# A decode step of attention and a gated FFN: the cache read by position blocks of one batch instead of by heads

## The chip, the core and the metric

The kernel runs on one core of a Trainium2 chip. The metric is device time in microseconds from one launch to its end; lower is better. Engines that matter here: PE (matmuls, with its weight loads PEld), DVE (elementwise work and reductions), ACT (copies out of PSUM, exponentials), SP (issues nearly all DMAs) and the 16 DMA engines that move HBM data into SBUF.

## The reference

Four batch rows, one new token each, 32 heads of 192, a cache of 8,192 positions of which the last W = 2,048 are used; D = 640, F = 1,536; everything is bfloat16.

```python
xn = layernorm(x)                                   # x: [4, 1, 640]
q = (xn @ wq) as [4, 32, 1, 192]                    # wq: [640, 6144]
k, v = k_cache[:, :, -W:, :], v_cache[:, :, -W:, :] # [4, 32, 2048, 192] each
p = softmax(q . k * 192 ** -0.5)
attn = (p . v) as [4, 1, 6144] @ wo                 # wo: [6144, 640]
ffn = (silu(xn @ w1) * (xn @ w3)) @ w2              # w1, w3: [640, 1536], w2: [1536, 640]
out = x + attn + ffn
```

The cache lies in HBM as [batch, head, position, 192]. K and V of the window are 201 of the 223 MB that the kernel reads, and each value is used once.

## The kernel before, in words

**Unit of work.** A unit is one head for all four batches. `load_k` and `load_v` (L105 to L113) bring 3 MB each: a partition is (position group q of 32, batch b), and holds 64 positions of 192, a run of 24,576 bytes in HBM. K and V have three buffers each (`kpool`, `vpool`); a load waits until the last reader of its buffer is done.

**Scores.** With one query row per head there is no matrix to multiply, so DVE multiplies K by the broadcast query (`mult`, L228, half a unit or 32 positions at a time), PE sums the products over the 192 elements by 12 accumulating matmuls with an identity (`adder`, L238, 512 columns of 32 positions by 16), and DVE reduces the last 16 (`reduce_tile`, L253). The query is broadcast over partitions by `q_bcast` (L221, L223).

**Softmax.** Per pair of heads: a maximum over a partition's columns (L258), a transpose by PE (L263), the maximum per batch (L268, L271), its broadcast by PE (L277, L279), the exponential on ACT (L283), and `chain_z` (L291), which spreads the weights of a partition over four columns, one for each batch, with zeros in the three that aren't its own. So 16 chains in all.

**Values.** `pv` (L313) multiplies z of eight positions (32 columns) by V of eight positions and 64 of the 192 elements (512 columns), three such column groups of 32 at once. Of the result only the diagonal blocks are wanted: `pick` (L323) masks on DVE and `pick_sum` (L331) adds. `fold` (L338, L344) sums over groups on PE and scales by the row sums; `ge_tr` and `ge_proj` (L350, L357) transpose four heads' result and multiply it by the 768 rows of Wo that belong to them (`wo_load`, L117, 7,680 bytes in a partition, eight times).

**What sets the order.** A table of slots (`sched`, L398 to L454): each stage has a slot number (two slots to a head) and a phase in it, and `behind` (L244) keeps DVE's small work behind the multiply of the same slot. SP's queue runs in program order, so a load that waits for a buffer holds up the loads behind it.

**Start and end.** Wq comes first (three loads, L136), then three K units. At the end: the last V, w1 and w3 (L365), the last Wo, and w2 in loads of 4, 4, 3 and 1 rows in a partition (L372). Behind the last landing stand two matmuls (L467), the final sum (L470) and two small stores (L472, L473).

Of the kernel before, what the change touches and what calls it, by code (L numbers as in the profile page):

```python
# [18 lines left out]
def kernel(  # L19
# [14 lines left out]
    HG: int = 4,  # L34
    QP: int = 8,
    KBUFS: int = 3,
    VBUFS: int = 3,
    PBUFS: int = 2,
    L: int = 7,
    ALIGN: int = 144,  # L40
):

# [12 lines left out]
    NQ = P // B  # L55
    NJ = W // NQ
# [4 lines left out]
    MASK = -30000.0  # L61
    NS = H * NC
    HH = 2
    PL = 32 // B
    DV = 512 // PL
    NV = Dh // DV
    RPP = (HG * Dh) // P
    OW = HG * Dh
    NCH = 512
    QW = 512  # L70
    QB = QP * Dh // QW
    FC = F // P
    DH = D // 2
    assert NJ % CH == 0 and CH * DD <= 512 and QP * Dh % QW == 0
    assert OW % P == 0 and Dh % RPP == 0 and H % HG == 0 and HG % HH == 0 and H % QP == 0 and QP % HH == 0
    assert NV * 32 <= P and NJ % (2 * PL) == 0 and DV * NV == Dh
    NG = P // 32
    NF = F // NCH
    CF = NCH // P
    NB = H * Dh // QW // NG  # L80
    assert H * Dh % (QW * NG) == 0 and NB <= 3
    assert DH <= 512 and F % NCH == 0 and NF <= NG

    const = ctx.enter_context(tc.tile_pool(name="const", bufs=1))
    kpool = ctx.enter_context(tc.tile_pool(name="kt", bufs=KBUFS))
    vpool = ctx.enter_context(tc.tile_pool(name="vt", bufs=VBUFS))
    wpool = ctx.enter_context(tc.tile_pool(name="wstream", bufs=2))
    ppool = ctx.enter_context(tc.tile_pool(name="pr", bufs=PBUFS))
    qpool = ctx.enter_context(tc.tile_pool(name="qbc", bufs=2))
    opool = ctx.enter_context(tc.tile_pool(name="o", bufs=2))  # L90
    small = ctx.enter_context(tc.tile_pool(name="small", bufs=3))
    ps_add = ctx.enter_context(tc.tile_pool(name="ps_add", bufs=2, space=MemoryType.PSUM))
    ps_o = ctx.enter_context(tc.tile_pool(name="ps_o", bufs=1, space=MemoryType.PSUM))
# [3 lines left out]
    kts, vts, prs, pss, scs, zts = {}, {}, {}, {}, {}, {}  # L97
    qbcs, wos, o_pss, rss, rcps, o_rs, o_bfs, chs = ({} for _ in range(8))
    mult_insts, es, o_ms = {}, {}, {}
    ORDER_DEP = mybir.DependencyInfo(mybir.DependencyClass.NoSync, mybir.DependencyReason.SCHED_ONLY)  # L100

    def cache_rows(cache, h):
        return cache[:, h, Sk - W:Sk, :].rearrange("b (q n) d -> q b (n d)", q=NQ)

    def load_k(j):  # L105
        kt = kpool.tile([P, NJ, Dh], BF16, tag="kt")
        nc.sync.dma_start(out=kt[:], in_=cache_rows(A_k_cache, j))
        kts[j] = kt

    def load_v(j):  # L110
        vt = vpool.tile([P, NJ, Dh], BF16, tag="vt")
        nc.sync.dma_start(out=vt[:], in_=cache_rows(A_v_cache, j))  # L112
        vts[j] = vt  # L113

    def wo_load(hg):
        wt = wpool.tile([P, RPP * D], BF16, tag="w")
        nc.sync.dma_start(out=wt[:], in_=A_wo[hg * OW:(hg + 1) * OW, :].rearrange("(p i) n -> p (i n)", i=RPP))  # L117
        wos[hg] = wt

    x_sb = ppool.tile([B, D], BF16, tag="pr")  # L120
    x_rows = A_x.rearrange("b s d -> (b s) d")
    nc.scalar.dma_start(out=x_sb[:], in_=x_rows)
# [7 lines left out]
    RV = NJ * Dh // (H * Dh)  # L130
    wq_rows = A_wq.rearrange("(p kc) n -> p kc n", kc=KC)
    wqs = []
    for r0 in range(0, KC, RV):
        r1 = min(r0 + RV, KC)
        wt = vpool.tile([P, RV, H * Dh], BF16, tag="vt")
        nc.sync.dma_start(out=wt[:, 0:r1 - r0, :], in_=wq_rows[:, r0:r1, :])  # L136
        wqs.append(wt)
    for h in range(KBUFS):
        load_k(h)
# [6 lines left out]
    nc.vector.memset(pad[:, 0:1], 0.0)  # L146
    nsc = const.tile([HH, HH], FP32, name="nsc")
    nc.vector.tensor_scalar_mul(out=nsc[:], in0=idf[0:HH, 0:HH], scalar1=-SCALE)
    selm = const.tile([P, B], FP32, name="selm")
    nc.vector.tensor_reduce(out=selm[:], in_=idf[:].rearrange("p (q b) -> p b q", b=B), axis=AX.X, op=ALU.add)  # L150
    selb = const.tile([P, B], BF16, name="selb")
    nc.vector.tensor_copy(out=selb[:], in_=selm[:])
    row = const.tile([P, 32], FP32, name="row")
    nc.vector.tensor_reduce(out=row[:], in_=idf[:].rearrange("p (g c) -> p c g", g=NG), axis=AX.X, op=ALU.add)
    fsel = const.tile([P, NV, B], FP32, name="fsel")
    nc.vector.tensor_reduce(out=fsel[:], in_=idf[:, 0:NV * 32].rearrange("p (k l b) -> p k b l", k=NV, l=PL), axis=AX.X, op=ALU.add)
    diag = const.tile([P, HH, PL], FP32, name="diag")
    for hh in range(HH):
        nc.vector.tensor_reduce(out=diag[:, hh, :], in_=row[:].rearrange("p (l b) -> p l b", b=B), axis=AX.X, op=ALU.add)
    oTs = []  # L160
    for i in range(2):
        oT = const.tile([P, RPP, 32], BF16, name=f"oT{i}")
        nc.gpsimd.memset(oT[:], 0.0)
        oTs.append(oT)

    xf = ppool.tile([B, D], FP32, tag="pr")
    nc.vector.tensor_copy(out=xf[:], in_=x_sb[:])
    ssum = const.tile([B, 1], FP32, name="ssum")
    nc.vector.tensor_reduce(out=ssum[:], in_=xf[:], axis=AX.X, op=ALU.add)
    negmean = const.tile([B, 1], FP32, name="negmean")  # L170
    nc.vector.tensor_scalar_mul(out=negmean[:], in0=ssum[:], scalar1=-1.0 / D)
    xc = ppool.tile([B, D], FP32, tag="pr")
    nc.vector.tensor_scalar_add(out=xc[:], in0=xf[:], scalar1=negmean[:, 0:1])
    ssq = const.tile([B, 1], FP32, name="ssq")
    nc.scalar.activation(out=xf[:], in_=xc[:], func=ACTF.Square, accum_out=ssq[:])
# [6 lines left out]
    xn = ppool.tile([B, D], BF16, tag="pr")  # L182
    nc.vector.tensor_scalar_mul(out=xn[:], in0=xc[:], scalar1=rstd[:, 0:1])

    xnT_ps = ps_t.tile([P, KC, B], BF16, tag="t")
    for kc in range(KC):
        nc.tensor.transpose(out=xnT_ps[:, kc, :], in_=xn[:, kc:D:KC], identity=idb[0:B, 0:B])
# [4 lines left out]
    sel = const.tile([P, NQ, B], BF16, name="sel")  # L192
    nc.vector.tensor_copy(out=sel[:], in_=selm[:].unsqueeze(1).to_broadcast([P, NQ, B]))

# [3 lines left out]
    for k in range(NB):  # L198
        if k < 2:
            qp = ps_add.tile([P, QW], FP32, tag="ps")  # L200
        else:
            qt = ps_o.tile([P, HH, QW], FP32, tag="o_ps")
            qp = qt[:, 0, :]
        q_pss.append(qp)
    for kc in range(KC):
        for k in range(NB):
            for g in range(NG):
                off = (k * NG + g) * QW
                nc.tensor.matmul(q_pss[k][32 * g:32 * g + 32, :], lhsT=xnT[:, kc, :],  # L209
                                 rhs=wqs[kc // RV][:, kc % RV, off:off + QW], start=(kc == 0), stop=(kc == KC - 1))  # L210
    q_sb = const.tile([P, NB, QW], BF16, name="q_sb")
    for k in range(NB):
        nc.scalar.copy(out=q_sb[:, k, :], in_=q_pss[k][:, :])

    def q_bcast(qg, m):
        k, g = (qg * QB + m) // NG, (qg * QB + m) % NG
        if m == 0:
            qbc = qpool.tile([P, QP, Dh], BF16, tag="qbc")
            qbcs[qg] = qbc
        bp = ps_t.tile([P, QW], FP32, tag="t")  # L220
        nc.tensor.matmul(bp[:], lhsT=sel[32 * g:32 * g + B].rearrange("k q b -> k (q b)"),  # L221
                         rhs=q_sb[32 * g:32 * g + B, k, :], start=True, stop=True)
        nc.scalar.copy(out=qbcs[qg][:].rearrange("p h d -> p (h d)")[:, m * QW:(m + 1) * QW], in_=bp[:])  # L223

    def mult(s):
        j, c = s // NC, s % NC
        pr = ppool.tile([P, CH, Dh], BF16, tag="pr")
        mi = nc.vector.tensor_tensor(out=pr[:], in0=kts[j][:, c * CH:(c + 1) * CH, :],  # L228
                                     in1=qbcs[j // QP][:, j % QP, :].unsqueeze(1).to_broadcast([P, CH, Dh]),
                                     op=ALU.mult)  # L230
        prs[s] = pr
        mult_insts[s] = mi

    def adder(s):
        ps = ps_add.tile([P, CH, DD], FP32, tag="ps")
        pr = prs.pop(s)
        for kk in range(NK):
            nc.tensor.matmul(ps[:], lhsT=idb[:], rhs=pr[:, :, kk * DD:(kk + 1) * DD],  # L238
                             start=(kk == 0), stop=(kk == NK - 1))
        pss[s] = ps  # L240

    slot = [0]

    def behind(inst):  # L244
        if slot[0] in mult_insts:
            tc.add_manual_dep(inst.ins, mult_insts[slot[0]].ins.name, ORDER_DEP, reason="vector engine issue order")

    def reduce_tile(s):
        j, c = s // NC, s % NC
        if s % (HH * NC) == 0:  # L250
            sc = small.tile([P, HH, NJ], FP32, tag="sc", bufs=2)
            scs[j // HH] = sc
        ri = nc.vector.tensor_reduce(out=scs[j // HH][:, j % HH, c * CH:(c + 1) * CH], in_=pss.pop(s)[:], axis=AX.X, op=ALU.add)  # L253
        behind(ri)
# [145 lines left out]
    def add(slot, phase, fn, *args):  # L400
        sched[slot].append((phase, len(sched[slot]), fn, args))
# [102 lines left out]
```

## Time and profile before

| | us |
|---|---|
| median of 3 runs (lowest to highest) | 527.16 (527.02 to 527.6) |
| the profiled execution's own time | 526.79 |
| its span, first to last instruction | 525.0 |
| PE busy, of the span | 326.4 |
| DVE busy | 328.3 |
| ACT busy | 39.6 |
| DMA: bytes moved, mean rate | 223.25 MB, 425 GB/s |

The profile is a page made from one execution. Its second part cuts the span into 40 slices of 13.1 us and gives each engine's busy share in tenths. Its third part lists the DMA queues, its fourth the chain of work that ended last, its fifth the groups of instructions by line: after the bar, the busy time in us and the mean ns of one, and after the second bar how long the engine had been idle before them and for whom it waited. The timeline gives start and length in us. The windows view gives, for each stretch, its length, the busy time of PE, PEld, DVE, ACT and POOL with counts, then the granted TensorE clock, the busy share of the DMA engines, and GB/s. The trace also holds a record of each DMA packet (start, length, bytes) and of the clock that the chip granted to PE.

### The profile page before, as it was taken

What the parts mean: (1) busy time and instruction counts of PE and PEld (TensorE: products, weight loads), DVE (VectorE), ACT (ScalarE), POOL (GpSimd) and SP (SyncE); (2) the same over time, 40 slices, a digit from 0 to 9 for tenths busy, and PEclk for the clock granted to TensorE, in tenths of its full rate; (3) what the DMA queues carried; (4) which work ended last, traced back from release to release, by engine and by line L of the source; (5) the groups of instructions that cost most, each with busy time, mean ns of one, the idle gap of its engine ahead of it and who ended that gap; (6) DMA issues with size and microseconds to landing.
All of it is one profiled execution on the core that took longest, in us unless ns stands there. A gap on an engine that the chain in (4) does not pass through costs nothing.

```text
span 525.0 us, 4658 instructions
## 1 busy us (share of the span) xinstructions
PE 326.4 (62%) x1991; PEld 142.2 (27%) x1991; DVE 328.3 (63%) x289; ACT 39.6 (8%) x121; POOL 1.8 (0%) x11
## 2 busy tenths in 40 slices
PE   2356376864758487662858566572857737585864
PEld 1122122321323133221324223231322313232432
DVE  3069455767757376865757486573758657575842
ACT  2300000100000010001000000100100000000121
POOL 1000000000000000000000000000000000000000
PEclk9999887786888778797878769797897868888889
DMA  8999999999999999999999999999999999999996
GB/s 360 433 436 428 431 436 426 438 426 433 431 432 432 433 434 427 436 429 429 439 424 434 429 435 426 438 422 439 434 430 429 430 434 434 430 433 430 426 428 256
DMA packets 11723, 223.25 MB, mean 425 GB/s; under 512 B 1316, under 2 KB 1464, under 8 KB 2872
## 3 DMA queue, kind: packets, MB, share of 16 engines
q1 hardware_dynamic: 11688, 222.97, 99.0%
q8 instruction: 15, 0.25, 0.2%
q14 instruction: 4, 0.03, 0.0%
q10 hardware_dynamic: 16, 0.01, 0.0%
HBM read 222.96 MB, written 0.01 MB: 425 GB/s over the span
## 4 chain that ended last, share of the span: by engine, by line
DMA 77%; DVE 13%; PE 8%; SPq 1%; issue 0%; DVEq 0%
DMA kt<-in_A_k_cache_dram 73%; DVE pr L228 11%; PE ps L238 6%; DMA w2t<-in_B_w_dram 5%; PE o_ps L313 1%; DVE sc L253 1%; SPq L112 0%; DVE o_r L331 0%; SPq L136 0%; DVE o_m L323 0%; PE acc L357 0%; SPq L372 0%; PE ft L467 0%; DVE z L291 0%; DVE res L470 0%
## 5 line engine op out<-in xcount | busy, mean ns | idle before, releaser
L238 PE MATMUL ps<-pr,idb 128*128 128x512 bf16 x768 | 223.7, 452 | 166.3 <-DVE pr L228 166.3
L228 DVE TENSOR_TENSOR pr<-kt,qbc 128x6144 bf16<-128x6144 bf16 x64 | 214.5, 3352 | 166.8 <-DMA kt<-in_A_k_cache_dram 166.8
L238 PEld LDWEIGHTS <-idb 128*128 128x128 bf16 x768 | 83.9, 112 | 285.1 <-issue 223.9
L313 PE MATMUL o_ps<-vt,z 128*32 128x512 bf16 x768 | 66.3, 389 | 1.2 <-DMA vt<-in_A_v_cache_dram 0.6
L253 DVE TENSOR_REDUCE sc<-ps 128x32 f32<-128x512 f32 x64 | 43.7, 683 | 6.8 <-PE ps L238 6.7
L313 PEld LDWEIGHTS <-z 128*32 128x32 bf16 x768 | 32.0, 98 | 28.3 <-issue 10.5
L331 DVE TENSOR_REDUCE o_r<-o_m 96x128 f32<-96x1024 f32 (+1 forms) x17 | 30.7, 1807 | 0.1
L283 ACT ACTIVATE e<-sc,negm 128x64 bf16<-128x64 f32 x32 | 10.9, 340 | 239.4 <-DVE negm L279 239.4
L323 DVE TENSOR_TENSOR o_m<-o_ps,diag 96x1024 f32<-96x1024 f32 (+1 forms) x17 | 19.5, 1148 | 7.6 <-PE o_ps L313 7.6
L344 ACT ACTIVATE o_bf<-fp,rcp 4x192 bf16<-4x192 f32 x32 | 11.4, 403 | 132.0 <-PE fp L338 132.0
L338 PE MATMUL fp<-o_r,fsel 96*4 96x128 f32 x96 | 13.1, 273 | 1.8 <-DVE o_r L331 1.8
L223 ACT CAST qbc<-bp 128x512 bf16<-128x512 f32 x12 | 6.8, 590 | 81.2 <-PE bp L221 81.2
L291 DVE TENSOR_TENSOR z<-e,selb 128x512 bf16<-128x512 bf16 x16 | 10.8, 678 | 0.9 <-ACT e L283 0.9
L209 PE MATMUL qp<-wt,xnT 128*32 128x512 bf16 x40 | 5.3, 623 | 8.2 <-DMA wt<-in_A_wq_dram 8.2
L338 PEld LDWEIGHTS fp<-o_r,fsel 96*4 96x4 f32 x96 | 7.1, 86 | 9.8 <-issue 5.5
L357 PE MATMUL acc<-wt,oT 128*32 128x320 bf16 x96 | 7.9, 301 | 0.8 <-DVE oT L351 0.8
L263 PE MATMUL mt<-idf,lmax 128*2 128x128 f32 x16 | 4.8, 301 | 5.5 <-DVE lmax L258 5.4
L277 PEld LDWEIGHTS mt<-nsc,gmq 2*128 2x128 f32 x32 | 4.7, 183 | 7.8 <-issue 6.4
L277 PE MATMUL mt<-nsc,gmq 2*128 2x2 f32 x32 | 6.1, 257 | 1.1 <-DVE gmq L271 1.1
L283 ACT ACTIVATION_READ_ACCUMULATOR e<-sc,negm 128x1 f32 x32 | 6.0, 187 | 0.0
L209 PEld LDWEIGHTS <-xnT 128*32 128x32 bf16 x60 | 2.4, 133 | 11.9 <-issue 11.0
L263 PEld LDWEIGHTS mt<-idf,lmax 128*2 128x2 f32 x16 | 1.3, 83 | 13.8 <-issue 8.1
(65 smaller groups left out, 69.9 us busy)
## 6 DMA issues: line engine op xcount, KB each, us to landing
kt<-in_A_k_cache_dram SPq DMA_DIRECT2D x32, 3072.0 KB, 34.3
vt<-in_A_v_cache_dram SPq DMA_DIRECT2D x32, 3072.0 KB, 32.4
wt<-in_A_wo_dram SPq DMA_DIRECT2D x8, 960.0 KB, 26.4
wt<-in_A_wq_dram SPq DMA_DIRECT2D x2, 3072.0 KB
wt<-in_B_w_dram SPq DMA_DIRECT2D x2, 1920.0 KB, 20.5
wt<-in_A_wq_dram SPq DMA_DIRECT2D x1, 1536.0 KB, 19.9
w2t<-in_B_w_dram SPq DMA_DIRECT2D x2, 640.0 KB
w2t<-in_B_w_dram SPq DMA_DIRECT2D x1, 480.0 KB
```

Of the source, the lines that this page charges most:

```text
L228: mi = nc.vector.tensor_tensor(out=pr[:], in0=kts[j][:, c * CH:(c + 1) * CH, :], in1=qbcs[j // QP][:, j % QP, :].unsqueeze(1).to_broadcast ...
L238: nc.tensor.matmul(ps[:], lhsT=idb[:], rhs=pr[:, :, kk * DD:(kk + 1) * DD], start=(kk == 0), stop=(kk == NK - 1))
L253: ri = nc.vector.tensor_reduce(out=scs[j // HH][:, j % HH, c * CH:(c + 1) * CH], in_=pss.pop(s)[:], axis=AX.X, op=ALU.add)
L277: nc.tensor.matmul(mt[:, P:P + HH], lhsT=gmq[:].rearrange("o q b -> o (q b)"), rhs=nsc[:], start=True, stop=True)
L283: nc.scalar.activation(out=e[:, hh, :], in_=sc[:, hh, :], func=ACTF.Exp, bias=negm[:, hh:hh + 1], scale=SCALE, accum_out=rs[:, hh:hh + 1])
L291: behind(nc.vector.tensor_tensor(out=z[:].rearrange("p h j b -> p (h j) b"), in0=e[:].rearrange("p h j -> p (h j)").unsqueeze(2).to_broadc ...
L313: nc.tensor.matmul(o_ps[32 * k:32 * k + 32, hh, :], lhsT=z[:, hh, g * PL:(g + 1) * PL, :].rearrange("p l b -> p (l b)"), rhs=vt[:, g * PL: ...
L323: behind(nc.vector.tensor_tensor(out=o_ms[u][:, h0:h1].rearrange("r h l d -> r (h l) d"), in0=o_pss[u][0:NV * 32, h0:h1, :].rearrange("r h ...
L331: behind(nc.vector.tensor_reduce(out=o_rs[u][:, h0:h1, :], in_=o_ms[u][:, h0:h1].rearrange("r h l d -> r h d l"), axis=AX.X, op=ALU.add))
L338: nc.tensor.matmul(fp[:, :, k * DV:(k + 1) * DV], lhsT=fsel[0:NV * 32, k, :], rhs=o_r[:], start=True, stop=True)
L344: nc.scalar.mul(out=o_bfs[hg][:, pr + hh, :], in_=fp[:, hh, :], mul=rcp[:, hh:hh + 1])
L357: nc.tensor.matmul(acc[32 * t:32 * t + 32, :], lhsT=oT[:, i, :], rhs=wo_t[:, i * D + t * DH:i * D + (t + 1) * DH], start=(hg == 0 and i == ...
```

## The change

A unit becomes 512 positions of one batch for all 32 heads: a partition is (head h, group r of 4), and holds 128 positions, a run of 49,152 bytes; a unit is 6 MB. K and V share one pool of three such buffers. There are 4 x 4 units of K and as many of V; the order of units is K of batch 0, then V of a batch and K of the next in turn, then V of batch 3. After each unit the next load is issued (`feed`). What follows from the layout:

- one query row per partition (`qb`), built once by windowed selection matmuls; four multiplies, adders and reduces to a K unit, as large as before; `keys` puts each reduce behind the next multiply, and after a K unit of batches 1 to 3 DVE reduces the last tile before it goes on;
- one softmax chain for each batch, on 512 columns, and its rows are written out one behind the other; all DVE and PE instructions are held in program order;
- `values`: z is 32 columns for each position (one for each head, zeros elsewhere), 128 x 4,096 in a unit; 64 matmuls of 64 columns (two positions) by 384 (two positions of V), in two column groups of 64. `pick` and `pick_sum` go; a batch's result is copied out by ACT (`evict`) and put in order by eight small float32 matmuls (`sort`);
- Wo is loaded once, 48 rows of 640 in a partition, in two loads of 10 and 38 rows, and projected once at the end. The last loads stand in this order: w1, w3, the last V unit in two halves, Wo's 10 rows, Wo's 38 rows, w2 in 8, 3 and 1 rows. On PE, behind the second-last V: the FFN's first matmuls and transposes, the two halves of the last V, `sort`, the 10 rows, the 38 rows, w2.

The core of the diff:

```diff
+    def load(which, b, s, n0=0, n1=NJ):
+        if n0 == 0:
+            kv = kvpool.tile([P, NJ, Dh], BF16, tag="kv")
+            kvs[which, b, s] = kv
+        p0 = Sk - W + s * NJ * R
+        rows = {"k": A_k_cache, "v": A_v_cache}[which][b, :, p0:p0 + NJ * R, :].rearrange("h (r n) d -> h r n d", r=R)
+        nc.sync.dma_start(out=kvs[which, b, s][:, n0:n1, :].rearrange("p n d -> p (n d)"),
+                          in_=rows[:, :, n0:n1, :].rearrange("h r n d -> h r (n d)"))
...
+    def keys(b, s):
+        for c in range(NC):
+            pr = mult(b, s, c)
+            reduces()
+            adder(b, s, c, pr)
...
+    def values(b, s, n0=0, n1=NJ):
+        n = n1 - n0
+        z = zpool.tile([P, H, n], BF16, tag="z")
+        at = s * NJ + n0
+        dve(nc.vector.tensor_tensor(out=z[:].rearrange("p h (a j) -> p h a j", j=ZB),
+                                    in0=es[b][:, at:at + n].rearrange("p (a j) -> p a j", j=ZB).unsqueeze(1).to_broadcast([P, H, n // ZB, ZB]),
+                                    in1=selz[:].unsqueeze(2).to_broadcast([P, H, n // ZB, ZB]), op=ALU.mult))
...
+        m, half = n // 4, n // 2
+        for j in range(m):
             for t in range(2):
+                a = t * m + j
+                pe(nc.tensor.matmul(o_pss[b][64 * t:64 * t + 64, 0:2 * Dh], lhsT=zf[:, a:a + (2 * H - 1) * half + 1:half],
+                                    rhs=vt[:, n0 + a:n0 + a + half + 1:half, :],
+                                    start=(s == 0 and n0 == 0 and j == 0), stop=(s == NU - 1 and n1 == NJ and j == m - 1)))
...
+    def proj(i0, i1):
+        for i in range(i0, i1):
+            for t in range(2):
+                pe(nc.tensor.matmul(acc[32 * t:32 * t + 32, :], lhsT=oT[:, i, :], rhs=wos[i][:, t * DH:(t + 1) * DH],
+                                    start=(i == i0 and i0 == proj0), stop=(i == proj1)))
...
+    def last_values():
+        for g in range(VS):
+            load("v", B - 1, NU - 1, g * NJ // VS, (g + 1) * NJ // VS)
+        wo_load(NI - WI, NI, ppool, "pr", [P, WI, D])
...
+    def last_weights():
+        wo_load(0, NI - WI, kvpool, "kv", [P, NJ, Dh])
+        for i0, i1 in ((0, (NF - 1) * CF), ((NF - 1) * CF, NF * CF - 1), (NF * CF - 1, NF * CF)):
+            w2_load(i0, i1)
+
+    units = [("k", 0, s) for s in range(NU)]
+    for b in range(B):
+        for s in range(NU):
+            units += [("v", b, s)] + ([("k", b + 1, s)] if b < B - 1 else [])
+    stream = [(load, u) for u in units[2:-1]] + [(gates, ()), (last_values, ()), (last_weights, ())]
...
+    feed()
+    for which, b, s in units[:-1]:
+        if which == "k":
+            keys(b, s)
         else:
+            if s == 0:
+                reduces()
+                chain(b)
+            values(b, s)
+        if stream:
+            feed()
+        if which == "k" and b > 0:
+            reduces()
...
+    ffn_mm(1)
+    ffn_mm(3)
+    ffn_transpose()
+    for g in range(VS):
+        values(B - 1, NU - 1, g * NJ // VS, (g + 1) * NJ // VS)
+    evict(B - 1)
+    sort(B - 1)
+    proj(NI - WI, NI)
+    proj(0, NI - WI)
```

## The prediction

> **What bounds the kernel now.** I read the slices of the span first, then the queues, then the costliest groups, then the timeline of the end. From the page, parts 2 to 4:
>
> ```profile
> DMA  8999999999999999999999999999999999999996
> GB/s 360 433 436 428 431 436 426 438 426 433 431 432 432 433 434 427 436 429 429 439 424 434 429 435 426 438 422 439 434 430 429 430 434 434 430 433 430 426 428 256
> q1 hardware_dynamic: 11688, 222.97, 99.0%
> DMA 77%; DVE 13%; PE 8%; SPq 1%; issue 0%; DVEq 0%
> ```
>
> The 16 DMA engines never rest between the first and the last slice, and SP's queue alone fills 99.0% of 16 engines' span: 519.7 us of packets. The first packet starts at 1.74 us and the last weight packet ends at 521.39 us (packet records of the trace), so there is no hole. The 13% of DVE in the chain is what happens to stand on it while transfers go on. The groups agree: the two biggest engines idle a third of the time, waiting for K.
>
> ```profile
> L238 PE MATMUL ps<-pr,idb 128*128 128x512 bf16 x768 | 223.7, 452 | 166.3 <-DVE pr L228 166.3
> L228 DVE TENSOR_TENSOR pr<-kt,qbc 128x6144 bf16<-128x6144 bf16 x64 | 214.5, 3352 | 166.8 <-DMA kt<-in_A_k_cache_dram 166.8
> L313 PE MATMUL o_ps<-vt,z 128*32 128x512 bf16 x768 | 66.3, 389 | 1.2 <-DMA vt<-in_A_v_cache_dram 0.6
> L253 DVE TENSOR_REDUCE sc<-ps 128x32 f32<-128x512 f32 x64 | 43.7, 683 | 6.8 <-PE ps L238 6.7
> L291 DVE TENSOR_TENSOR z<-e,selb 128x512 bf16<-128x512 bf16 x16 | 10.8, 678 | 0.9 <-ACT e L283 0.9
> ```
>
> So three things can move the time: the length of the packets, a transfer that starts late, and what runs after the last landing. The timeline of the end shows the third:
>
> ```profile
> 517.57 0.99 PE L357 MATMUL acc<-wt,oT 128*32 128x320 bf16 x12
> ...
> 518.63 0.72 PE L467 MATMUL ft<-w2t,hT 128*32 128x320 bf16 x8
> ...
> 520.17 0.72 PE L467 MATMUL ft<-w2t,hT 128*32 128x320 bf16 x8 [0.81 <-DMA w2t<-in_B_w_dram]
> 520.17 0.50 PEld L467 LDWEIGHTS <-hT 128*32 128x32 bf16 x8 [1.03 <-issue]
> 521.31 0.72 PE L467 MATMUL ft<-w2t,hT 128*32 128x320 bf16 x8 [0.42 <-DMA w2t<-in_B_w_dram]
> 521.31 0.50 PEld L467 LDWEIGHTS <-hT 128*32 128x32 bf16 x7 [0.64 <-issue]
> 522.07 0.48 DVE L470 TENSOR_TENSOR res<-ft,attn_bf 64x320 bf16<-64x320 f32 x1 [2.63 <-PE ft L467]
> ```
>
> Everything is projected before the last weights land; `res` starts 0.68 us after the last packet's end (521.39), and 2.9 us later the span ends. That last part stays.
>
> **Packets: the gain.** The bytes are the same (223 MB). By the packet records a packet of 24,576 B takes 912 ns, 12,288 B 460, 7,680 B 291, 1,280 B 55. From 12,288 to 24,576 B that is 452 ns for 12,288 B; 912 less two times 452 leaves 8 ns that a packet costs whatever its size (the two small sizes fit: 282 + 8, 47 + 8). A load gives each engine 8 of its 128 packets. Per engine, K and V now have 512 packets; then 31 units give 248 of 49,152 B and the last V, halved, 16 of 24,576 B: 248 fewer. Wq 24 to 16, Wo 64 to 16, w2 32 to 24: 64 fewer. 312 x 8 ns = 2.50 us. Each DMA also ends in a 9 ns packet on each engine, and the queue's loads go from 81 to 42: 0.35 us. **Gain 2.85 us**, if a 49,152 B run goes as one packet, which no row shows: nearest row the 24,576 B one, and if the run is cut into two of those, the gain falls to 0.7 us (256 + 8 packets more per engine).
>
> **Late transfers: none, with 3.5 us to spare at the tightest.** A unit is now 8 packets x 1.816 us = 14.5 us of DMA, and three buffers mean that the load of unit u+3 waits for unit u's last reader. By the slope: Wq ends at 1.74 + 14.5 + 3.7 = 19.9 us, keys 0 to 3 of batch 0 land at 34.5, 49.0, 63.5 and 78.1, then V0 at 92.6, K1 at 107.1, the next V at 121.7. A key unit is 4 multiplies of 3.35 us and 4 reduces of 0.68 us on DVE, 16.1 us, its adders (48 matmuls, 216 ns apart at full clock, 10.4 us) beside it. First unit from 34.9 with PE's half clock: its last multiply ends at about 51.2; then 16.1 us each: 67.3, 83.5, 99.6. Each is before the third landing after it (78.1 for the first: the queue is never empty). The softmax chain of the batch now stands alone in DVE's order: last adder 2.7, reduce 0.7, then (rows L258, L268, L271, L279, L283, scaled to 512 columns) about 4 us: 107. Then z: 4,096 elements. By L228's rate 2.3 us (in both rows the last dimension is what differs: 192 in a row there, a step of 0 in L291; here 16 in a row, so L228 is nearer); by L291's 8 x 678 ns = 5.4 us. I take 2.3. Values: 64 matmuls of 384 columns in two column groups of 64. L313 shows three groups of 32 at once: one group of 512 columns every 0.217 us at full clock, 0.427 at half. 32 pairs are then 5.2 us, and about 7.3 us from a cold start; one after another 10.4 us. With pairs V0 is read at 117, and its successor's load is only due when the queue runs dry at 121.7: 3.5 us left after an issue of 1 us. From then on a pair of units takes 2.4 us for z, 5.3 for the values with two multiplies beside them, and 15 for the rest: the first adder stands behind the values on PE, and the new wait at the end, the last reduce for the last adder, holds up the next z, which is queued behind it on DVE. About 23 us against 29.1 us of DMA, so the slack grows. The 30.7 and 19.5 us of `pick_sum` and `pick` on DVE go, 16 x 2.3 us of z comes: off the path both ways. In the last batch V follows V with 14.5 us for 2.3 + 5.3 us of work.
>
> The Trainium skill, DMA: Bandwidth & Descriptors, Latency and other measured facts, speaks against the change: HBM copies lose rate when lock-step streams stand large powers of two apart (207 GB/s at 512 KiB, 164 at 2 MiB, against 214 padded). Before, neighbouring row groups of one load lie 24 KB apart; afterwards, its heads lie 3 MiB apart. If loads lost 3 to 23% as there, an estimate is 14 to 140 us more; no run here shows that pitch, and I keep it out of the sum.
>
> **The end: the loss.** The order of the last loads is w1 and w3, V in halves, 10 rows of Wo, 38 rows of Wo, w2 in 8 + 3 + 1 rows. PE's order is the FFN's first matmuls, the halves, evict, sort, 10 rows projected, 38 rows projected, then w2. DMA ends 2.85 us earlier, at E. The w2 packets take 8 x (385 + 149 + 55 ns) = 4.7 us, and a landing is seen about 0.36 us after its packet (3,840 B packets end at 520.97, matmuls start at 521.31). So the 38 rows are seen at E - 4.36. By then the last half of V (18.4 us before) and all that follows from it (z made before it lands, 16 pairs 2.6, evict 0.6, sort 1.2, 10 pairs 1.4) has been over for about 10 us. PE has idled and starts at half clock:
>
> ```profile
> 487.00:491.00 4.00, 3.74 (x10) 1.38 (x10) 4.00 (x6) 0.77 (x4) 0.00 (x0) 0.52 1.00 430
> ...
> 510.00:525.00 15.00, 7.64 (x91) 4.07 (x91) 3.92 (x8) 3.62 (x7) 0.00 (x0) 1.00 0.66 275
> ```
>
> These are stages of the windows view; the third figure from the end is the granted clock: 0.52 in the 4 us after an idle PE (its adders came 427 ns apart), 1.00 in the old end, where PE never paused long. Over the 27 restarts in the trace the full clock came 2.7 to 5.7 us after the first matmul, 4.0 on average: half of that, 2.0 us (1.4 to 2.9), is lost. At full clock a pair of 320-column matmuls goes every 135 ns (LDWEIGHTS of L357 at 517.585, 517.720, 517.856). 38 + 12 = 50 pairs: 49 x 0.135 = 6.6 us to the last start, then 0.35 us to `res` (521.72 to 522.07). `t1` (0.48 + 0.32 us on DVE) is hidden by the 12 pairs of w2; without them it would be 0.8 us late. `res` starts at E - 4.36 + 2.0 + 6.6 + 0.35 = E + 4.6, where it was E + 0.7: **loss 3.9 us** (3.3 to 4.8).
>
> **Sum.** 3.9 - 2.85 = +1.05 us on the profiled execution: span 525.0 to 526.05, its time 526.79 to 527.84. The median shown is 527.16, 0.37 us above that execution, so the median becomes **528.2 us**. 0.2%, about what a measurement of this kernel can tell from no change, is 1.05 us: my forecast lies on that edge, a little slower or nothing. Own range, from the loss's own bounds, 527.6 to 529.1.
>
> **Rivals.**
> 1. Not slower: PE keeps its clock at the end. For it: the gate's phase shifts from restart to restart by 3 us; if idle time before w2 is filled or the gate opens at the first pair, 2.0 us fall away. Against: all 27 restarts took at least 2.7 us. Net -0.95: 526.2 us. It decides from a loss at the end below 2.85 us, that is a restart under 1.9 us.
> 2. The 48 KB run is cut into two packets: +3.9 - 0.7 = +3.2 us: 530.4 us. For it: no longer packet than 24,576 B among the loads; against: every load in the trace goes as one packet per row.
> 3. The values starve the queue: column groups of 64 do not run together (10.4 us) and z goes at 5.4 us. A pair of units is then 5.4 + 10.4 + 15 = 31 us against 29.1, 12 pairs: +23 us and 4 us at V0: 555 us. For it: only groups of 32 are seen. It decides when z and values together pass 14 us.
> 4. Packets slow down with heads 3 MiB apart. Each 1% on K and V is 4.65 us: at 1 to 3%, 533 to 542 us. For it: no row has the pitch; against: all 8,448 of the 24,576 B packets stay close to 912 ns, whatever array they read.
>
> **Chances.** Forecast 0.64, rival 1 0.10, rival 2 0.08, rival 3 0.07, rival 4 0.11. The range: 526.2 (rival 1) to 533.0 (rival 2 and the start of rival 4) leaves out rival 3 and most of 4, and a little below rival 1: less than 0.2. The forecast is split by the edge, 0.31 same and 0.31 slower, with 0.02 faster for a short restart; rival 1 is 0.05 faster and 0.05 same; the other 0.26 are slower. Faster 0.07, same 0.36, slower 0.57.
>
> **What would show it.** Right: DMA at 0.99 or more in every middle slice and about 433 GB/s (49,152 B in 1.816 us, 16 engines); queue packets near 336 x 16 and their endings; an idle PE before the 38 rows, a clock near half behind it, and `res` some 4.6 us after the last packet. Wrong: holes in the DMA slices, SP waiting for PE at a V load past the third landing, K packets longer than 1.82 us, or PE warm at the end.

## The result

The median went from 527.60 us (five runs beside it, 527.02 to 527.71) to **529.63 us** (five runs, 529.30 to 529.93): ratio 1.0041, 95% interval 1.0027 to 1.0056. A second set on another occasion gave 1.0051 (1.0038 to 1.0063). So the change costs 2 to 2.7 us. The forecast was 528.2, range 526.2 to 533.0, likeliest verdict "slower by over 0.2%". The five runs of the kernel before lie in two groups, 527.02 to 527.16 and 527.60 to 527.71, and this time the median is of the upper one; the forecast started from 527.16, and 529.63 is 2.5 us above that, not 1.05.

The page of the changed kernel, parts 2 to 5:

```profile
DMA  8999999999999999999999999999999999999992
GB/s 358 444 445 421 432 452 422 421 434 451 419 421 460 429 425 434 444 422 425 444 438 421 432 452 425 426 436 441 421 429 449 429 422 440 445 401 441 435 427 120
q1 hardware_dynamic: 6072, 222.96, 98.0%
...
L279 PE MATMUL o_ps<-kv,z 128*64 128x384 bf16 x1024 | 114.5, 396 | 51.8 <-DVE z L267 43.0
...
L267 DVE TENSOR_TENSOR z<-e,selz 128x4096 bf16<-128x4096 bf16 (+1 forms) x17 | 36.7, 2158 | 16.9 <-PE o_ps L279 13.2
```

The DMA row is still full in every slice but the ends: the larger units starve nothing. SP's queue now needs 6,072 packets in place of 11,688. What changed is the last slice: 120 GB/s where it was 256. The transfers end earlier in it and the span ends later. The timeline of the end (start us, length us, engine):

```profile
505.71 2.85 PE L311 MATMUL acc<-wt,oT 128*32 128x320 bf16 x20 [0.65 <-ACT oT L297]
516.16 6.76 PE L311 MATMUL acc<-wt,oT 128*32 128x320 bf16 x76 [7.60 <-DMA wt<-in_A_wo_dram]
...
522.74 1.80 PE L419 MATMUL ft<-ft,hT 128*32 128x320 bf16 x24
...
524.59 0.48 DVE L422 TENSOR_TENSOR res<-ft,t 64x320 bf16<-64x320 f32 x1 [0.80 <-PE ft L419]
```

PE waits 7.6 us for Wo's 38 rows (their last packet ends at 515.79), then runs 76 + 24 matmuls without a pause. The last packet of all ends at 520.44 us by the packet records; the final sum starts 4.15 us later. Three stages of the same stretch, in the windows view (the third figure from the end is PE's granted clock):

```profile
508.60:516.10 7.50, 0.00 (x0) 0.00 (x0) 0.00 (x0) 0.00 (x0) 0.00 (x0) 0.73 0.92 393
516.16:519.10 2.94, 2.94 (x24) 1.91 (x25) 0.00 (x0) 0.00 (x0) 0.00 (x0) 0.50 0.67 274
519.10:523.00 3.90, 3.90 (x60) 3.16 (x58) 0.04 (x1) 0.00 (x0) 0.00 (x0) 1.00 0.09 34
```

There are 24 matmul records in the first 2.94 us at clock 0.50 and 60 in the next 3.9 us at 1.00: this is the restart at half clock, 2.93 us of it (the clock records change to full at 519.09).

### The profile page after: what moved, and what is told of

Its sections match the earlier page's. It is cut to its first block, busy times and chain, and to the rows that moved or that the text cites. A ratio compares the mean times of both kernels' runs of the same rounds, so it can differ in the third digit from the quotient of the medians.

```text
span 527.4 us, 4688 instructions
## 1 busy us (share of the span) xinstructions
PE 342.5 (65%) x2147; PEld 201.3 (38%) x2147; DVE 300.5 (57%) x189; ACT 17.8 (3%) x34; POOL 3.5 (1%) x11
## 3 DMA queue, kind: packets, MB, share of 16 engines
q1 hardware_dynamic: 6072, 222.96, 98.0%
## 4 chain that ended last, share of the span: by engine, by line
DMA 50%; DVE 27%; PE 21%; issue 1%; ACT 0%; SPq 0%; DVEq 0%; ACTq 0%
DMA kv<-in_A_k_cache_dram 38%; DVE pr L211 20%; PE o_ps L279 9%; PE ps L218 9%; DMA wt<-in_A_wo_dram 7%; DMA kv<-in_A_v_cache_dram 5%; DVE sc L228 4%; DVE z L267 3%; PE acc L311 1%; PE fp L295 1%; ACT e L251 0%; PE ft L419 0%; PE mt L246 0%; DVE gmax L243 0%; DVE lmax L239 0%
## 5 line engine op out<-in xcount | busy, mean ns | idle before, releaser
L211 DVE TENSOR_TENSOR pr<-kv,qb 128x6144 bf16<-128x6144 bf16 x64 | 213.4, 3351 | 106.1 <-DMA kv<-in_A_k_cache_dram 106.1
L218 PE MATMUL ps<-pr,idb 128*128 128x512 bf16 x768 | 194.1, 410 | 97.0 <-DVE pr L211 97.0
L218 PEld LDWEIGHTS <-idb 128*128 128x128 bf16 x768 | 79.2, 103 | 209.1 <-issue 124.4
L279 PE MATMUL o_ps<-kv,z 128*64 128x384 bf16 x1024 | 114.5, 396 | 51.8 <-DVE z L267 43.0
L279 PEld LDWEIGHTS <-z 128*64 128x64 bf16 x1024 | 96.4, 198 | 69.3 <-DVE z L267 52.7
L267 DVE TENSOR_TENSOR z<-e,selz 128x4096 bf16<-128x4096 bf16 (+1 forms) x17 | 36.7, 2158 | 16.9 <-PE o_ps L279 13.2
L195 PE MATMUL qp<-wq,xnT 128*32 128x384 bf16 x80 | 6.3, 506 | 8.1 <-DMA wq<-in_A_wq_dram 8.1
L311 PEld LDWEIGHTS <-oT 128*32 128x32 bf16 x96 | 6.5, 118 | 11.2 <-issue 8.7
L295 PEld LDWEIGHTS fp<-o_ev,esel 128*128 128x128 f32 x64 | 7.7, 192 | 1.3 <-ACT o_ev L287 0.9
L295 PE MATMUL fp<-o_ev,esel 128*128 128x48 f32 x64 | 7.6, 273 | 0.6 <-ACT o_ev L287 0.6
## 6 DMA issues: line engine op xcount, KB each, us to landing
kv<-in_A_v_cache_dram SPq DMA_DIRECT2D x15, 6144.0 KB, 27.7
```

Source lines behind the costliest of these rows:

```text
L195: pe(nc.tensor.matmul(q_pss[k][32 * g:32 * g + 32, 0:QW], lhsT=xnT[:, kc, :], rhs=wq[:, 2 * k:2 * k + 2, g, :], start=(kc == 0), stop=(kc ...
L211: dve(nc.vector.tensor_tensor(out=pr[:], in0=kvs["k", b, s][:, c * CH:(c + 1) * CH, :], in1=qb[:, b, :].unsqueeze(1).to_broadcast([P, CH, ...
L218: pe(nc.tensor.matmul(ps[:], lhsT=idb[:], rhs=pr[:, :, kk * DD:(kk + 1) * DD], start=(kk == 0), stop=(kk == NK - 1)))
L267: dve(nc.vector.tensor_tensor(out=z[:].rearrange("p h (a j) -> p h a j", j=ZB), in0=es[b][:, at:at + n].rearrange("p (a j) -> p a j", j=ZB ...
L279: pe(nc.tensor.matmul(o_pss[b][64 * t:64 * t + 64, 0:2 * Dh], lhsT=zf[:, a:a + (2 * H - 1) * half + 1:half], rhs=vt[:, n0 + a:n0 + a + hal ...
L295: pe(nc.tensor.matmul(fp[:], lhsT=esel[:, t, R - 1 - c:R - 1 - c + P], rhs=o_ev[:, t, c * NI:(c + 1) * NI], start=(c == 0 and t == 0), sto ...
```

## The experiments

E below is the end of the last packet in the profiled execution, "tail" the time from E to the start of the final sum; both are from the packet records and the timeline. Ratios are against the kernel before, run on the same chip.

| kernel | median us (runs) | ratio, 95% interval | E | tail |
|---|---|---|---|---|
| before (first profile / again) | 527.1 | 1 | 521.39 / 521.57 | 0.69 / 0.66 |
| changed | 529.63 (5) | 1.0041 (1.0027 to 1.0056) | 520.44 | 4.15 |
| changed, again | 529.79 (5) | 1.0051 (1.0038 to 1.0063) | 520.40 | 4.76 |
| halves | 531.25 (5) | 1.0075 (1.0063 to 1.0087) | 521.68 | 4.79 |
| quarters | 533.92 (4) | 1.0121 (1.0106 to 1.0135) | 524.43 | 5.33 |
| wo4 | 527.45 (11) | 0.9996 (0.9987 to 1.0004) | 520.46 | 1.52 |
| warm | 528.56 (12) | 1.0026 (1.0016 to 1.0037) | 520.48 | 4.41 |
| warm44 | 528.16 (9) | 1.0028 (1.0017 to 1.0040) | 520.62 | 4.78 |
| wo4warm | 527.18 (12) | 0.9998 (0.9989 to 1.0007) | 521.80 | 0.80 |
| touter | 532.07 (4) | 1.0109 (1.0085 to 1.0133) | 525.00 | 2.61 |
| wo4w2 | 526.28 (11) | 0.9982 (0.9973 to 0.9991) | 520.45 | 0.89 |
| wqhalf | 530.04 (1) | one run | 519.96 | 5.51 |
| best | 525.89 (11) | 0.9978 (0.9969 to 0.9987) | 520.14 | 0.84 |

### The price of a packet: halves and quarters

```diff
+        cuts = 2 if n1 - n0 == NJ else 1        # quarters: 4
+        m = (n1 - n0) // cuts
+        for a in range(n0, n1, m):
+            nc.sync.dma_start(out=kvs[which, b, s][:, a:a + m, :]..., in_=rows[:, :, a:a + m, :]...)
```

> The changed kernel with every whole K and V unit loaded by two DMAs of 24,576 B runs in place of one of 49,152 B: 248 packets and 31 endings more on each DMA engine, nothing else. Theory P, the prediction's price, a packet costs 8 ns beyond its bytes: 248 x 8 = 2.0 us and 31 x 9 ns = 0.3 us more than the changed kernel's 529.6, so 531.9. Theory O, the packets' records overlap by some 4 ns, so that half of the 8 ns was never spent: 1.0 to 1.3 us more, 530.8. Theory W, run length does nothing and the 1 us by which the DMA ended earlier comes from elsewhere (Wo, the start): 529.6.

> The same with four DMAs of 12,288 B runs: 744 packets and 93 endings more on each engine. Theory P: 6.0 + 0.8 = 6.8 us more, 536.4. Theory O: 3.0 + 0.4 = 3.4 us more, 533.0. Theory W: 529.6.

The windows view of 60 to 460 us (last figure: GB/s), quarters, then halves, then the changed kernel, then the kernel before:

```profile
60.00:460.00 400.00, 265.45 (x1572) 160.43 (x1571) 255.45 (x147) 6.09 (x14) 0.00 (x0) 0.87 1.01 429
```

```profile
60.00:460.00 400.00, 269.76 (x1584) 159.49 (x1584) 258.83 (x149) 6.10 (x14) 0.00 (x0) 0.89 1.00 432
```

```profile
60.00:460.00 400.00, 274.96 (x1571) 153.30 (x1571) 264.26 (x151) 6.10 (x14) 0.00 (x0) 0.88 1.00 433
```

```profile
60.00:460.00 400.00, 254.89 (x1507) 110.88 (x1507) 263.21 (x217) 24.28 (x89) 0.00 (x0) 0.82 1.01 432
```

The DMA is full in all of them, and the rate falls as the runs get shorter. E moves by 1.24 us for 248 packets and 31 endings, and by 2.75 us for the next 496 and 62: 5.0 and 5.5 ns a packet with its share of the endings, 4 to 4.5 ns without. That is theory O, not the prediction's 8 ns, nor theory W. The medians alone would not decide it: 531.25 and 533.92 us lie between theory O (530.8, 533.0) and theory P (531.9, 536.4), since the tail grew as well, to 4.79 and 5.33 us. The packet records agree with O: behind a 24,576 B packet the same engine's next record starts, most often, 4 ns before that record's end. So about half of the 8 ns in a record's length is overlap and was never time.

### The projection at the end: wo4, wo4w2

```diff
+    WOC = ((0, 10), (10, 20), (20, 30), (30, NI - WI))
...
+        for a0, a1 in WOC if i0 == 0 else ((i0, i1),):
+            nc.sync.dma_start(out=flat[:, (a0 - i0) * D:(a1 - i0) * D], in_=...[:, a0:a1, :]...)
```

wo4w2 moreover loads w2 in 4, 4, 3 and 1 rows.

> The changed kernel with Wo's 38 rows in loads of 10, 10, 10 and 8 in place of one. The theory (the end is 50 pairs of matmuls that wait for one landing): the first 30 rows are projected as they land, behind the last landing of Wo stand 8 pairs and w2's, and the last matmuls wait for w2 alone: the final sum starts 0.7 to 1.2 us after the last packet in place of 4.15, so 3.0 to 3.4 us less, 526.4 us, below the kernel before. Rival: the projection isn't what ends late (w2's matmuls or the final sum are), or the three more landings cost as much: within 0.5 us of 529.6.

> The kernel wo4 with w2 in loads of 4, 4, 3 and 1 rows (as in the kernel before) in place of 8, 3 and 1. In wo4's profile the final sum started 1.5 us after the last packet, because w2's first 8 rows come as one landing and PE is at half clock there. The theory: the first four rows are multiplied while the rest lands, the final sum starts 0.8 to 1.1 us after the last packet without extra matmuls, 0.5 us less than wo4: 526.6 to 526.9 against 527.1 of the kernel before. Rival: the last two cluster times of wo4 come from elsewhere: 527.4 again.

The end of wo4, then of wo4w2, in the timeline:

```profile
516.19 2.32 PE L314 MATMUL acc<-wt,oT 128*32 128x320 bf16 x16 [1.39 <-DMA wt<-in_A_wo_dram]
...
519.23 2.71 PE L422 MATMUL ft<-ft,hT 128*32 128x320 bf16 x24 [0.72 <-DMA ft<-in_B_w_dram]
521.98 0.48 DVE L425 TENSOR_TENSOR res<-ft,t 64x320 bf16<-64x320 f32 x1 [2.60 <-PE ft L422]
```

```profile
516.14 2.32 PE L314 MATMUL acc<-wt,oT 128*32 128x320 bf16 x16 [1.12 <-DMA wt<-in_A_wo_dram]
518.22 3.08 PE L422 MATMUL ft<-ft,hT 128*32 128x320 bf16 x24
...
521.34 0.48 DVE L425 TENSOR_TENSOR res<-ft,t 64x320 bf16<-64x320 f32 x1 [2.02 <-PE ft L422]
```

With the same E, 16 matmuls stand behind Wo's last landing in place of 76, and the tail falls from 4.15 to 1.52 us. wo4 gained 2.2 us in the median (529.63 to 527.45; 2.4 by the ratios), not the 3.0 to 3.4 expected: its runs lie in two clusters (four at 525.9 to 526.7, seven at 527.3 to 527.7). The profile is of the lower one, and even there w2's first landing is multiplied at half clock (up to 521.12 us); that the upper cluster has more of the same is inferred, as no run of it was profiled. With w2 as in the kernel before, its first matmuls run while the rest lands (518.22), the tail is 0.89 us, all eleven runs lie between 525.95 and 526.72, and the kernel is faster than before: 0.9982.

### The clock in the pause: warm, warm44, wo4warm

```diff
     proj(NI - WI, NI)
+    for w in range(WARM):            # 28; warm44: 44
+        dm = ps_t.tile([P, 512], FP32, tag="t")
+        pe(nc.tensor.matmul(dm[:], lhsT=idb[:], rhs=selz[:]..., start=True, stop=True))
     proj(0, NI - WI)
```

> The changed kernel with 28 extra 128x512 matmuls (their result is not used) between the 10 rows and the 38 rows, while PE waits for Wo. The theory (PE falls to half clock in that pause and runs 3 us at half): the 38 rows start at full clock and 1.5 us go, 528.1. Rival: the clock isn't what makes the projection long (its weights or PSUM are): 529.6 or a little more.

> The kernel warm with 44 extra matmuls in place of 28, which reach nearly to the landing of Wo's 38 rows. The run of warm had two clusters (527.5 to 527.8 and 529.3 to 529.7), and its profiled execution, of the upper one, still paused 4.35 us. The theory: with a pause of a microsecond every execution starts the 38 rows at full clock: one cluster at 527.6. Rival: the extra matmuls don't decide, two clusters remain.

> The kernel wo4 with 6, 9, 9 and 8 extra 128x512 matmuls (result not used) behind the four pieces of the projection, so that PE never pauses long before w2. The theory: with a full clock only the last two rows of w2 stand behind the last landing, the final sum starts 0.7 to 0.9 us after the last packet in every execution, 525.9 us, 1.2 us under the kernel before, and the two clusters of wo4 (525.9 to 526.7, 527.3 to 527.7) become one. Rival: the clusters come from something else than PE's clock: two clusters remain, median about 527.

warm fell into two clusters, 527.5 to 527.8 (six runs) and 529.3 to 529.7 (six). Its profile is of the upper one (529.64) and shows the pause left over; the profile of warm44, also of its upper cluster (530.02), shows no pause:

```profile
505.65 6.22 PE L411 MATMUL dm<-selz,idb 128*128 128x512 bf16 x28
516.21 7.01 PE L312 MATMUL acc<-wt,oT 128*32 128x320 bf16 x76 [4.35 <-DMA wt<-in_A_wo_dram]
```

```profile
508.02 10.43 PE L411 MATMUL dm<-selz,idb 128*128 128x512 bf16 x44
518.39 5.34 PE L312 MATMUL acc<-wt,oT 128*32 128x320 bf16 x76
```

The same 76 matmuls take 7.01 us after a pause of 4.35 us, with the granted clock at 0.50 up to 520.32, and 5.34 us right behind other work at clock 1.00: the clock costs 1.7 us there. warm44's expectation failed in its detail: in that execution part of the extra work itself ran at half clock and passed Wo's landing by 2 us, so two clusters remain (527.8 to 528.3, six runs; 529.7 to 530.0, three). The lower clusters are 1.3 to 2.1 us below the changed kernel's 529.63, about the price that the clock was given; no run of them was profiled, so that the clock made them is inferred from this size. Neither length of filler brought all runs into the lower cluster.

The clock records show where two clusters can come from. In each of the 14 profiles the granted clock changes only at whole multiples of 3.41 us from its other changes, and the place of this grid in the program differs from execution to execution. So the same restart can meet the next change sooner or later: Wo's matmuls start at 516.1 to 516.2 us in both profiles of the changed kernel, and the full clock comes at 519.09 in one and 520.31 in the other. An estimate from that: one step more at half clock costs half of 3.41, or 1.7 us, which is about the distance between the clusters.

wo4warm has the tail of 0.80 us that was expected, and no gain: E is 521.80. Fifteen engines end by 520.03 and one at 521.80. The packet records show a 16 KB instruction fetch at 519.7 on DMA, where wo4 has none; beside such a fetch a data packet takes about 0.5 us longer (49,152 B: 2.28 to 2.37 us for 1.815, in all 14 places of the changed kernel). The likely reading is that the extra instructions brought the fetch forward and paid on the queue what they saved on PE. It is not shown: the records don't number the engines, 1.3 us is more than the 0.5 of the other places, and best, without extra matmuls, has a fetch at 520.1, just as its last packet ends.

### Column groups and the slack of the queue: touter

```diff
-        for j in range(m):
-            for t in range(2):
+        for t in range(2):
+            for j in range(m):
```

> The changed kernel with the two loops of the values exchanged: 32 matmuls of the first column group, then 32 of the second, so that neighbours can't run side by side. The theory (pairs of 64-column groups run at once, and the loads have little slack at the first V): a value unit goes from 6.8 to about 11 to 12 us, its load is issued 4 to 5 us later, and the queue begins to run dry: 0 to 6 us more than 529.6. Rival (the groups of 64 never ran together): values stay at 6.8 us, time unchanged.

The first value unit in the timeline of the changed kernel, then of touter, and touter's GB/s by slices:

```profile
108.83 7.41 PE L279 MATMUL o_ps<-kv,z 128*64 128x384 bf16 x64 [3.42 <-DVE z L267]
...
116.27 0.54 SPq L109 DMA_DIRECT2D kv<-in_A_k_cache_dram  x1
```

```profile
109.01 12.14 PE L279 MATMUL o_ps<-kv,z 128*64 128x384 bf16 x64 [3.42 <-DVE z L267]
...
121.18 0.54 SPq L109 DMA_DIRECT2D kv<-in_A_k_cache_dram  x1
```

```profile
GB/s 360 445 439 415 448 439 412 445 439 367 448 439 415 435 445 424 430 446 423 434 443 426 426 453 423 424 452 426 416 460 424 423 439 434 426 418 335 450 435 157
```

The same matmuls, only in another order, take 12.1 us in place of 7.4: neighbouring matmuls on the two column groups of 64 do run at once. The load behind the first V goes out 4.9 us later, and slices of 367 (119 to 133 us of its span of 530.5) and 335 GB/s (477 to 491 us, V behind V) are holes; the changed kernel's lowest middle slice is 401. E is 4.6 us later. Part of that comes back: PE, busier, runs the projection at full clock (5.34 us), and the tail is 2.61 us.

### Where the rest of the DMA's gain went: before again, changed again, wqhalf

```diff
-    nc.sync.dma_start(out=wq0, in_=wq_rows[:, 0:RV, :])
+    for r0 in range(0, RV, 2):
+        nc.sync.dma_start(out=wq0[:, r0:r0 + 2, :], in_=wq_rows[:, r0:r0 + 2, :])
```

> The kernel before, unchanged, for a second profile. In the three profiles with 49,152 B runs that end in the same loads the last packet ends at 520.44 to 520.48 us. If that of before (521.39) is as steady, the transfers gained 0.9 us; if it moves by several tenths, the gain has that uncertainty.

> The changed kernel, unchanged, beside the others on the same chip: 529.6 us, 1.0041 of before, and the last packet at 520.4 to 520.6 us.

> The changed kernel with Wq's first four rows in two loads of 24,576 B runs, as before, in place of one of 49,152 B: a look at the last packet's end alone. The first packet of each engine takes 0.72 us more than a later one of 49,152 B, and took 0.59 us more at 24,576 B. If the transfers' missing gain (0.6 us) lies in the start, the last packet ends 0.1 to 0.6 us before 520.45; if not, at 520.4 to 520.6.

E is steady: 521.39 and 521.57 before, 520.40 to 520.62 in the four profiles that share the changed kernel's loads. By E the transfers gained 0.8 to 1.2 us. At 4.2 ns for 312 packets and 9 ns for 39 endings they should have gained 1.31 + 0.35 = 1.66.

E is the end of the slowest of 16 engines. The last load's 1,280 B packets stand eight to an engine, one right behind the other, so their records can be joined into engines. The mean of the 16 ends is 519.97 and 520.01 us before, and 518.52 in both profiles of the changed kernel: the mean engine gained 1.5 us, nearly what the price of a packet promises. What E lacks is mostly the lag of the slowest engine, 1.4 to 1.6 us behind the mean before and 1.9 afterwards.

wqhalf ends at 519.96, 0.46 us earlier, for 24,576 B runs in the first load alone; its mean end is 518.42, only 0.1 earlier. So the large first load seems to weigh on the slowest engine. One execution shows this; `best` points the same way with less (520.14 against wo4w2's 520.45). wqhalf's own time was not better, its tail was the longest of all (restart at half clock, up to 521.43 us).

### Both mended: best

> wo4w2 and wqhalf together: the projection and w2 in pieces at the end, Wq's first rows in two loads at the start. The theory (the two parts of the loss are independent): the last packet ends at 519.9 to 520.1 and the final sum starts 0.9 us later: 525.8 us, 0.9975 of before, 0.4 under wo4w2. Rival: the gain of wqhalf was one execution's: 526.3.

The end in the timeline of best:

```profile
515.81 1.26 PE L315 MATMUL acc<-wt,oT 128*32 128x320 bf16 x16 [1.50 <-DMA wt<-in_A_wo_dram]
...
520.10 0.84 PE L423 MATMUL ft<-ft,hT 128*32 128x320 bf16 x8 [0.51 <-DMA ft<-in_B_w_dram]
520.98 0.48 DVE L426 TENSOR_TENSOR res<-ft,t 64x320 bf16<-64x320 f32 x1 [3.03 <-PE ft L423]
```

The median is 525.89 us, ratio 0.9978 (0.9969 to 0.9987): 1.1 us faster than the kernel before and 3.7 faster than the change as made. That it beats wo4w2 (0.9982) can't be told from these intervals. In this execution the clock stood at 1.00 from 508.93 us past the final sum, in wo4w2's at 0.50 up to 520.82, and the tails are alike (0.84 and 0.89): with the end cut this way, these two executions do not show the clock in the tail.

## Why the prediction was right, and which term was off

- **Bound and rivals.** Right: the DMA stays full, so only packets, late transfers and the end could count.
- **The range.** It held by its width: its upper part was there for rivals 2 and 4, and neither came true. The range worked out from the loss alone, 527.6 to 529.1, did not hold 529.63. The direction and the mechanism (an earlier end of the DMA, a later end of PE) were right.
- **"Gain 2.85 us".** This is the step that was mis-sized; the transfers end 0.95 us earlier (520.44 for 521.39). A 49,152 B run goes as one packet (1,815 ns against 1,816 forecast, 6,072 packets), so rival 2 fell. But "912 less two times 452 leaves 8 ns that a packet costs" took a record's length for its cost: halves and quarters give 4 to 4.5 ns. The check to make was there before: an engine's 648 packets and 81 endings at their record lengths come to 519.7 us, as much as the whole stretch from first to last packet (519.6), though engines start up to 0.8 us late and seven of them end 2.5 us early or more. The second part is the slowest engine, which ends 0.3 to 0.5 us further behind the mean than before; the sum had one mean engine. wqhalf ties it to the first load, in one execution.
- **"Late transfers: none".** Right: values of the first V end at 116.2 us (forecast 117), z takes 2.28 us (2.3), a value unit 5.5 to 8.3. Landings were later than forecast: K1 is seen at 110.45 us, not 107.1, as the slowest engine of 16 counts and the model had one mean engine (the 16 endings of that load come at 107.55 to 110.05, 108.20 on average). That error was on the safe side, since it leaves the buffers more time. Rival 3 was a real mechanism: touter puts z and values at 14.4 us, past the stated 14, and holes appear, at a price of 4.6 us of E. The 27 us stated were for z at 5.4 us as well, which no run shows; with z at the 2.3 us measured, the rival's own sum for a pair of units is 2.3 + 10.4 + 15 = 27.7 us against 29.1, so no loss in its 12 pairs; touter's two holes lie at the first V and where V follows V.
- **"Loss 3.9 us".** 3.5 us in the first profile (tail 4.15 for 0.69), 4.1 in the second. From the start of Wo's 76 matmuls to the final sum the forecast was 2.0 + 6.6 + 0.35 = 8.95 us; measured 8.43 and 9.05, and 7.01 in warm44 at full clock (6.95 forecast without the restart). wo4 shows that the projection behind one landing is the cause, warm beside warm44 that the clock is about 1.7 us of it.
- **Rival 1** (PE keeps its clock) fell as it stood: both profiles of the changed kernel show the restart, and none of its ten runs (529.30 to 530.19) lies lower; half the runs of warm come 1.8 to 2.1 us lower, about the price it was given. The gain being smaller, it would not have made the change faster either.
- **Rival 4**, and the Trainium skill's row on rows of HBM large powers of two apart (DMA: Bandwidth & Descriptors, Latency and other measured facts): not seen. The 3,968 whole packets of K and V, with heads 3 MiB apart, take 1,815 ns in the median and 1,817 on average, and the stretch moves 433 GB/s, 432 before. halves is the cleanest test: its runs are as long as those of the kernel before and its heads 3 MiB apart, and both show 432 GB/s and 912 ns a packet. That row is measured on copies at other pitches; here loads at 3 MiB lose nothing.
- **The sum.** +1.05 forecast, +2.4 in the two profiled spans and +2.03 in the medians: of the profile's 2.4, -0.95 is E, +3.46 the tail, and -0.1 what stands behind the final sum. So in these two profiles the gain was 1.9 us smaller than forecast and the loss 0.4 us smaller, and by luck the second error hid a part of the first.

## What to carry to other kernels

On a kernel whose DMA queues never rest, longer runs can win only the fixed part of each packet, and that part must be taken from how far E or the rate moves, not from a packet record's length: records overlap. What is worth more is what stands behind the last landings: gather no work behind one large landing, cut the last weights so that each piece is used while the next one lands, and count matmuls after a long pause of PE at half clock. Reckon the end of the transfers by the slowest of the 16 engines, not by a mean one. A large first transfer and an instruction fetch beside the last loads each went with a later end here, in one profile each; they are worth a trial, not yet a rule.

## What the runs showed of the hardware

- A DMA packet costs about 4 ns beyond its bytes (27.2 B/ns on each engine), and a DMA's ending has a record of 9 ns on each engine; 12,288, 24,576 and 49,152 B runs give 429, 432 and 433 GB/s.
- The 16 engines do not end together: in the changed kernel seven end at 516.6 to 517.4 us and nine at 518.8 to 520.4, in the kernel before seven at 518.2 to 518.9 and nine at 520.2 to 521.4. What waits for a load waits for the slowest one.
- The first packets of the program are long: 24,576 B take 1.1 to 1.9 us instead of 0.91, and 49,152 B 1.8 to 2.9 instead of 1.82.
- A 16 KB instruction fetch makes the data packet beside it about 0.5 us longer; in wo4warm, one at the very end goes with an E 1.3 us later.
- PE's full clock came 2.7 to 5.7 us after a restart in the kernel before and 2.8 to 5.9 in the changed one. In all 14 profiles the clock changes on a grid of 3.41 us, which lies differently in each execution; the runs of wo4, warm and warm44 fell into clusters whose middles are 1.4 to 2.0 us apart.
